# Late stores, diagonal copies, k and v in parts, and other zero products in an attention and MLP kernel

## The chip, the core and the metric

One core of one Trainium2 chip. The time is that of the whole program on the device, in microseconds (us), as the median of several executions. Engine names: PE is TensorE, PEld its weight loads, DVE VectorE, ACT ScalarE, POOL GpSimd, SPq the queue that issues DMAs. L68 and L74 are helpers that record nearly every VectorE, ScalarE and GpSimd operation (L68) and nearly every product (L74), so one goes by the names of tiles.

## The reference

Landmark attention on 8 batches of 8 heads (576 positions of 64, 32 landmarks), then a two-layer network with a layer norm and a residual on the 4608 rows of 512 that come out. What matters here is the inverse of the 32 x 32 matrix of each head, by six Newton steps:

```python
A, Bm, C = sm(q, k_lm), sm(q_lm, k_lm), sm(q_lm, k)
Z = Bm.T / (norm1(Bm) * norminf(Bm) + 1e-6)          # for each head
for _ in range(6):
    Z = 2 * Z - Z @ Bm @ Z
x = A @ Z @ C @ v                                    # then x + relu(ln(x) @ w1) @ w2
```

## The kernel before

The two parts run interleaved: while one set of batches goes through the attention, the rows of earlier batches go through the network ("MLP"), in groups. A product of the MLP is a long row of 128x128x512 matmuls (psh, pso), and these fill TensorE. The Newton steps are short and depend on each other, so each one is set between stretches of MLP products. A step of a set of W units (four heads each) is this (cut: reshapes, and `bmbd`, a second block diagonal that is built after the last step; the first batch multiplies 32x32 blocks and needs no `ebd`):

```python
for it in range(6):
    lo = 0 if it < 5 else LM                                   # LM = 32, D = 64
    psn = p1([P, W, LM + D], "psn")                            # PSUM
    for w in range(W):
        MM(psn[:, w, lo:], ebd[:, w, :, :], st[:, w, lo:])     # four heads in one product
    stn = asm.tile([P, W, LM + D], FP16, name="st", tag="st")
    dve.scalar_tensor_tensor(out=stn[:, :, lo:], in0=st[:, :, lo:], scalar=2.0,
                             in1=psn[:, :, lo:], op0=ALU.mult, op1=ALU.subtract)
    st = stn
    if it < 5:
        ebd = diagonal("ebd", st[:, :, 0:LM], W, masks(W))
    # ... products of the scores, and (by "yield") products of the MLP ...
```

`ebd` is the block diagonal of four 32x32 matrices that lie on four quarters of the partitions. It is made by one multiplication with a mask:

```python
def diagonal(name, src, W, mask):
    t = asm.tile([P, W, 4, LM], FP16, name=name, tag=name, bufs=1)
    dve.tensor_tensor(out=t[:], in0=src[:, :, None, :].broadcast_to([P, W, 4, LM]),
                      in1=mask, op=ALU.mult)
    return t
```

Meanwhile GpSimd converts the next q, k and v to 16 bits (nat, natv) and adds q up to landmarks (asum). At the beginning TensorE has nothing to do until the first loads have landed, and is kept busy with products of zeros (in this trace they start 107 ns apart up to 5.2 us and 56 ns apart after it, and the granted clock is full from 5.2 us on):

```python
def warm(n, cols):
    idle = psM.tile([P, 512], FP32, name="idle", tag="pm")
    for _ in range(n):
        MM(idle[:, 0:cols], zeros[:], zeros[:, None, :].broadcast_to([P, cols // P, P]))
# ...
warm(50, 128)
```

The softmax here doesn't subtract the row's maximum and nothing guards it: scores larger than these inputs give would overflow.

Of the kernel before, what the change touches and what calls it, by code (L numbers as in the profile page):

```python
# [9 lines left out]
FP16 = mybir.dt.float16  # L10
# [3 lines left out]
ALU = mybir.AluOpType  # L14
AX = mybir.AxisListType

P = 128
# [3 lines left out]
def kernel(  # L21
# [55 lines left out]
    def TR(o, i_, idn):  # L77
        keep(nc.tensor.matmul(o, i_, idn, is_transpose=True, tile_position=(0, 0)))


    def load(src, b, u, queue):
        t = stage.tile([P, 2, NJ, D], FP32, name="stg", tag="stg")
        keep(queue.dma_start(
            out=t[:],
            in_=src[b, 4 * u:4 * u + 4].rearrange("(r e) (t j) d -> (e t) r j d", e=2, j=NJ)))
        return t
# [3 lines left out]
    def load_qk(b):  # L90
        for u in range(U):
            raw[b]["q", u] = load(q, b, u, nc.sync)
            raw[b]["k", u] = load(k, b, u, nc.sync)

    def load_v(b):
        for u in range(U):
            raw[b]["v", u] = load(v, b, u, nc.sync)

# [11 lines left out]
    def cast_qk(b, u, nm, engine):  # L110
        t = nat.tile([P, NJ, 2, D], FP16, name="nat", tag="nat")
        engine.tensor_copy(out=t[:].rearrange("p j r d -> p r j d"), in_=raw[b][nm, u][:])
        nat_tiles[b, nm, u] = t
# [51 lines left out]
    maskw = const.tile([P, 4, 4], FP16, name="maskw")  # L165
    mask16 = const.tile([P, 4], FP16, name="mask16")
    nc.gpsimd.tensor_copy(out=mask16[:], in_=mask4[:])
    for w in range(4):
# [21 lines left out]
    pool.tensor_copy(out=natv_buf[0][:, 0:2, :, 0:D], in_=raw[0]["v", 0][:])  # L190
    pool.tensor_copy(out=natv_buf[0][:, 2, :, 0:D], in_=raw[0]["v", 1][:, 0])
    bones = const.tile([P, 4, 32], FP16, name="bones")
    for u in range(U):
# [87 lines left out]

    def diagonal(name, src, W, mask):
        t = asm.tile([P, W, 4, LM], FP16, name=name, tag=name, bufs=1)
        dve.tensor_tensor(out=t[:], in0=src[:, :, None, :].broadcast_to([P, W, 4, LM]),
                          in1=mask, op=ALU.mult)
        return t

    def masks(W):
        return mask16[:, None, :, None].broadcast_to([P, W, 4, LM])


    def attention(bs):
# [13 lines left out]
        for w, (b, u) in enumerate(units):  # L306
            for i, nm in enumerate(("q", "k")):
                n16 = nat_tiles[b, nm, u]
                pst = p2([P, NJ, P], FP16, "pst")

                def sums():
                    for j in range(NJ):
                        MM(pss[:, i, w, :], n16[:, j, :, :].rearrange("p r d -> p (r d)"),
                           pm16[:], start=(j == 0), stop=(j == NJ - 1), skip=True)

                last = (w, i) == (W - 1, 1)
                if last:
                    sums()
                for j in range(NJ):
                    TR(pst[:, j, :], n16[:, j, :, :].rearrange("p r d -> p (r d)"), ident16[:])  # L320
                t = aprep.tile([P, NJ, P], FP16, name="xT", tag="xT" + nm, bufs=5 if nm == "q" else 4)
                if not first and i == 1:
                    dve.tensor_copy(out=t[:], in_=pst[:])
                elif not (first and last):
                    scalar.copy(t[:], pst[:])
                xT[nm, w] = t
                if not last:
                    sums()
                yield
# [10 lines left out]
        if first:  # L340
            dve.tensor_copy(out=t[:], in_=pst[:])
        yield
# [34 lines left out]
        psse_ = p1([P, 4, W * LM], "psse")  # L377
        psse = psse_[:, 0:2, :].rearrange("p a (u l) -> p a u l", u=W)
        for w in range(W):
            for h in range(4):  # L380
                sl = ds(32 * h, 32)
                MM(psse[sl, 1, w, :], bmT[sl, w, :], bmT[sl, w, :], rb=32 * h, cb=32 * h)
        MM(psse[:, 0, :, :], bones[:].rearrange("p a c -> p (a c)"), bm16[:])
        dve.tensor_reduce(out=psse_[:, 2, 0:W], in_=psse[:, 0, :, :], axis=AX.X,
# [9 lines left out]
        if not first:  # L394
            ebd = diagonal("ebd", st[:, :, 0:LM], W, masks(W))

# [3 lines left out]
        for w, (b, u) in enumerate(units):  # L400
            natv = natv_of[b]
            for j in range(NJ):
                for h in range(4):
                    r, e = divmod(h, 2)
                    rows = ds(64 * e, 64)
                    MM(pscv[ds(32 * h, 32), w, :], ect[w][rows, j, ds(32 * r, 32)],
                       natv[rows, 2 * u + r, j, :], rb=64 * e, cb=32 * h,
                       start=(j == 0), stop=(j == NJ - 1), skip=True)
        rcv = asm.tile([P, W], FP32, name="rcv", tag="rcv")
# [7 lines left out]
        for it in range(6):  # L417
# [16 lines left out]
            if not first and it < 5:  # L434
                ebd = diagonal("ebd", st[:, :, 0:LM], W, masks(W))
            if it < W:
# [168 lines left out]
    def attention2(bs, c):  # L605
# [39 lines left out]
        for w in range(W):  # L645
            for h in range(4):
# [11 lines left out]
                                op=ALU.mult)  # L658
        ebd = diagonal("ebd", st[:, :, 0:LM], W, masks(W))


        pscv = ps2.tile([P, 2, 512], FP32, name="pscv", tag="p2")
        for y in range(W // 2):
# [13 lines left out]
            if y + 1 < W // 2:  # L677
                yield
        v_used.update(c.bs)
        pcv = pscv[:, :, 0:(W // 2) * (D + 1)].rearrange("p x (y e) -> p y x e", e=D + 1)  # L680
        rcv = asm.tile([P, W], FP32, name="rcv", tag="rcv")
# [10 lines left out]
        for it in range(6):  # L692
# [9 lines left out]
            if it < 5:  # L702
                ebd = diagonal("ebd", st[:, :, 0:LM], W, masks(W))
            else:
                bmbd = diagonal("bmbd", bm16, W,
                                maskw[:, 0:W, :, None].broadcast_to([P, W, 4, LM]))
            if it < W // 2:
# [168 lines left out]
    def mlp():  # L876
        for g in range(NGRP):
# [44 lines left out]
            for u in range(4):  # L922
# [5 lines left out]
                for m in range(MCH):  # L928
# [4 lines left out]
                    if g == 0 and u >= 2 and m % 8 == 3:  # L933
                        n = len(turned.get(1, ()))
                        if 4 + n in xn_of:
# [4 lines left out]
                                         in1=x_blk.pop(j)[:], op0=ALU.mult, op1=ALU.add)  # L940
                store(j, ot)
                yield True

    stream = mlp()

    def fill(n):
        for _ in range(n):
            if not next(stream, False):
                return


# [5 lines left out]

    warm(50, 128)
    for _ in range(4):
        run(a0)  # L960
        warm(3, 256)
    run(a0)
    warm(1, 512)
    run(a0)
    scalar.copy(natv_buf[0][:, 3, :, 0:D], raw[0]["v", 1][:, 1])
    warm(1, 512)
# [71 lines left out]
    for i, _ in enumerate(a1):  # L1038
        fill(5 if i < 9 else 7)
        settle()  # L1040
        next_cast()
        if 5 <= i < 11:
            sets[0].next_job()
# [8 lines left out]
    for c, after, count in zip(sets, sets[1:] + [None], counts):  # L1052
        for step, _ in enumerate(attention2(c.bs, c)):
            fill(count[step])
            settle()
            if late and step >= 3:
# [6 lines left out]
        while after and (after.jobs or after.lms):  # L1063
            fill(8)
            next_cast()
            after.next_job()
    for _ in stream:
        pass

# [29 lines left out]
```

## Time and profile before

| | before |
|---|---|
| time, median of 3 (range) | 329.57 us (328.33 to 330.2) |
| PE busy, products recorded | 96% of the span, 3409 |
| first psn; first product of MLP group 3 | 15.31 us; 141.71 us |
| waits of psn and its weight load on ebd | 1.6 + 4.4 us |

The prediction below shows the lines for this, and places from the timeline (start us, us, engine, line, operation, out<-in). This is from the page's list of costliest groups; after the count come busy time in us, mean ns of one, and idle time of the engine before them:

```profile
L68 DVE TENSOR_TENSOR ebd<-st,mask 128x256 f16<-128x256 f16 (+1 forms) x30 | 20.7, 690 | 1.0
```

And this is one place from the timeline of the kernel before (start us, us, engine, line, operation, out<-in):

```profile
47.55 1.15 POOL L68 CAST nat<-stg 128x1152 f16<-128x1152 f32 x1 [0.90 <-DMA stg<-in_k_dram]
48.11 0.86 DVE L68 TENSOR_TENSOR ebd<-st,mask 128x256 f16<-128x256 f16 x1
48.97 1.15 POOL L68 CAST nat<-stg 128x1152 f16<-128x1152 f32 x1 [0.27 <-DVE ebd L68]
```

The half-size ebd takes 0.42 us where GpSimd is idle. Here it starts inside a GpSimd cast that runs until 48.70, and ends 0.27 us after it: it takes 0.86 us, since it waits for the cast. That the next cast starts when ebd has ended doesn't show that GpSimd waits too: 0.26 to 0.29 us lie between two casts here also where no ebd is in the way (before 50.40 in this kernel). Where GpSimd did wait is seen in the additions that the prediction lists.

### The profile page before, as it was taken

Reading aid. Unit: us, or ns where it says so; the run is one execution under the profiler, and the core shown is the slowest. Engines: PE = TensorE matmul, PEld = TensorE weight load, DVE = VectorE, ACT = ScalarE, POOL = GpSimd, SP = SyncE. Lnnn points to the kernel's source line nnn. Section 1 sums busy time; section 2 is a strip of 40 time slices with the busy share of each in tenths; the row PEclk is TensorE's granted clock in tenths of the full one; section 3 lists DMA queues with packets and bytes.
Section 4 is the critical chain, followed back from the end, with each engine's and each line's share of the span. In section 5 each row is a group of like instructions: output and inputs, shape, how many; then the busy total and the mean of one; then the engine's idle time right before and its main releaser. Section 6 shows DMA issues by size and latency. Waiting matters only on the chain.

```text
span 327.9 us, 8249 instructions
## 1 busy us (share of the span) xinstructions
PE 314.7 (96%) x3409; PEld 162.3 (50%) x3409; DVE 175.7 (54%) x395; ACT 152.7 (47%) x307; POOL 153.3 (47%) x241
## 2 busy tenths in 40 slices
PE   8889999999999999989999999999999999999995
PEld 8547864553445444435544445454444444444444
DVE  3668769779964797953237668722566120010012
ACT  3546762749960661957204672454046107305600
POOL 3389979999999999999800034100014000000000
PEclk9999999999999999999999999999999999999998
DMA  7999999898797864695022103330242126032023
GB/s 278 394 356 365 366 402 303 297 345 239 241 195 231 234 169 127 156 290 102 4 68 66 34 20 76 82 50 2 64 104 26 32 64 98 0 72 60 0 49 79
DMA packets 36397, 50.34 MB, mean 154 GB/s; under 512 B 17796, under 2 KB 22152, under 8 KB 36360
## 3 DMA queue, kind: packets, MB, share of 16 engines
q1 hardware_dynamic: 36200, 49.69, 52.7%
q8 instruction: 26, 0.43, 0.5%
q10 hardware_dynamic: 160, 0.13, 0.2%
q14 instruction: 11, 0.09, 0.1%
HBM read 36.70 MB, written 9.44 MB: 141 GB/s over the span
## 4 chain that ended last, share of the span: by engine, by line
PE 56%; POOL 22%; DMA 7%; issue 2%; ACT 2%; DVE 1%; SPq 0%; POOLq 0%
PE psh L74 26%; PE pso L74 25%; POOL asum L68 11%; POOL nat L68 6%; POOL natv L68 3%; DMA stg<-in_q_dram 3%; POOL xn L68 2%; DMA w2stg<-in_moe_w_ch_dram 2%; POOL s L68 1%; PE psy L74 1%; PE pscv L74 1%; DMA stg<-in_v_dram 1%; DMA stg<-in_k_dram 1%; DMA xnT<-xn 1%; ACT xn L68 1%
## 5 line engine op out<-in xcount | busy, mean ns | idle before, releaser
L74 PE MATMUL psh<-xnT,w 128*128 128x512 f16 (+1 forms) x640 | 133.7, 358 | 1.4 <-DMA xnT<-xn 1.4
L74 PE MATMUL pso<-w,hT 128*128 128x512 f16 (+1 forms) x592 | 132.9, 374 | 0.0
L68 ACT ACTIVATE hT<-psh 128x512 f16<-128x512 f32 x144 | 84.9, 597 | 97.6 <-PE psh L74 97.4
L74 PEld LDWEIGHTS <-w 128*128 128x128 f16 x640 | 59.5, 98 | 56.7 <-issue 3.1
L74 PEld LDWEIGHTS <-hT 128*128 128x128 f16 x592 | 56.1, 98 | 57.2 <-issue 0.8
L68 DVE SCALAR_TENSOR_TENSOR ot<-pso,rstd,xblk 128x512 f32<-128x512 f32 (+1 forms) x37 | 27.1, 732 | 77.6 <-PE pso L74 77.4
L68 POOL CAST nat<-stg 128x1152 f16<-128x1152 f32 x28 | 32.5, 1167 | 3.4 <-DMA stg<-in_k_dram 1.7
L68 POOL TENSOR_TENSOR asum<-asum 128x256 f32<-128x256 f32 (+2 forms) x54 | 28.4, 527 | 4.2
L68 DVE TENSOR_TENSOR xblk<-psy,rcpd 128x512 f32<-128x512 f32 (+1 forms) x40 | 27.6, 691 | 1.8 <-POOL w L68 0.2
L68 POOL TENSOR_TENSOR asum<-nat 128x576 f32<-128x576 f16 x18 | 23.4, 1299 | 1.5
L68 POOL TENSOR_SCALAR xn<-xblk,mvg 128x512 f16<-128x512 f32 x14 | 9.6, 694 | 30.9 <-ACT junk L68 30.9
L68 DVE SCALAR_TENSOR_TENSOR st<-st,psn 128x192 f16<-128x192 f16 (+3 forms) x36 | 14.2, 395 | 17.6 <-PE psn L74 17.4
L68 POOL CAST natv<-stg 128x1152 f16<-128x1152 f32 (+1 forms) x16 | 17.6, 1119 | 9.6 <-DMA stg<-in_v_dram 9.6
L68 POOL TENSOR_SCALAR negm<-mvg 128x1 f32<-128x1 f32 x14 | 2.7, 191 | 40.5 <-DVE mvg L68 35.9
L68 DVE TENSOR_TENSOR ebd<-st,mask 128x256 f16<-128x256 f16 (+1 forms) x30 | 20.7, 690 | 1.0
L68 DVE STREAM_TRANSPOSE xT<-nat 128x576 uint32<-128x576 uint32 x24 | 18.2, 760 | 2.2 <-POOL nat L68 2.2
L74 PE MATMUL psy<-zcbd,ea 128*128 128x260 f16 (+1 forms) x80 | 15.9, 276 | 1.0 <-DVE xblk L68 0.4
L68 ACT ACTIVATE ea<-psea 128x576 f16<-128x576 f32 x12 | 7.2, 648 | 16.5 <-PE psea L74 16.5
L74 PE MATMUL idle<-zeros 128*128 128x128 f16 (+2 forms) x82 | 13.4, 312 | 1.1 <-DVE eps_ln L172 1.1
L74 PEld LDWEIGHTS <-ea 128*128 128x128 f16 (+1 forms) x80 | 7.1, 100 | 12.2 <-issue 3.5
L68 ACT ACTIVATE junk<-xblk 128x512 f16<-128x512 f32 x14 | 8.8, 625 | 9.4 <-DVE xblk L68 9.2
L68 DVE BATCH_NORM_STATS2 st<-xblk 128x6 f32<-128x512 f32 x18 | 12.4, 688 | 0.5
(115 smaller groups left out, 263.0 us busy)
## 6 DMA issues: line engine op xcount, KB each, us to landing
stg<-in_q_dram SPq DMA_DIRECT2D x16, 576.0 KB, 6.0
stg<-in_k_dram SPq DMA_DIRECT2D x16, 576.0 KB, 5.7
out_dram<-ot SPq DMA_DIRECT2D x70, 128.0 KB, 2.4
stg<-in_v_dram SPq DMA_DIRECT2D x10, 576.0 KB, 6.4
w1stg<-in_moe_w_ch_dram SPq DMA_DIRECT2D x16, 256.0 KB, 6.0
w2stg<-in_moe_w_ch_dram SPq DMA_DIRECT2D x16, 256.0 KB, 5.2
stg<-in_v_dram SPq DMA_DIRECT2D x12, 288.0 KB, 5.5
xnT<-xn SPq DMA_TRANSPOSE x28, 3.3
```

What stands on the lines that cost most here:

```text
L68: return lambda *args, **kw: keep(getattr(self.engine, op)(*args, **kw))
L74: keep(nc.tensor.matmul(o, l, r, start=start, stop=stop, tile_position=(rb, cb), skip_group_check=(skip or cb != 0)))
```

## The change

Its intent, as I read it: shorter VectorE work in the Newton steps (plain copies into a matrix whose other blocks stay zero, instead of a multiplication over all four blocks), stores that don't stand in front of the transposes on the DMA queue, an earlier start, and fewer instructions for the warm-up. The core of the diff (cut: the changed order of some products of the first batch, the casts and copies of the last k and v in parts, the earlier `bmbd`, three more zero products left out after the first batch's steps and one shortened, and the bookkeeping of the stores):

```diff
+halves = ((slice(0, 2), slice(0, 5)), (slice(0, 2), slice(5, NJ)))
+pairs = ((slice(0, 1), slice(0, NJ)), (slice(1, 2), slice(0, NJ)))
-            raw[b]["k", u] = load(k, b, u, nc.sync)
+            raw[b]["k", u] = load(k, b, u, nc.sync, halves if (b, u) == (0, U - 1) else whole)
-            raw[b]["v", u] = load(v, b, u, nc.sync)
+            raw[b]["v", u] = load(v, b, u, nc.sync, pairs if (b, u) == (0, U - 1) else whole)
 ...
+    ebd = const.tile([P, 4, 4, LM], FP16, name="ebd")
+    nc.gpsimd.memset(ebd[:], 0.0)
 ...
-    def diagonal(name, src, W, mask):
-        t = asm.tile([P, W, 4, LM], FP16, name=name, tag=name, bufs=1)
-        dve.tensor_tensor(out=t[:], in0=src[:, :, None, :].broadcast_to([P, W, 4, LM]),
-                          in1=mask, op=ALU.mult)
-        return t
+    def diagonal(src, W):
+        for h in range(4):
+            rows = ds(32 * h, 32)
+            dve.tensor_copy(out=ebd[rows, 0:W, h, :], in_=src[rows, :, :])
 ...
-                store(j, ot)
+                if at_end:
+                    store(j, ot)
+                else:
+                    to_store.append((j, ot))      # stored after the next transposes are issued
 ...
-    warm(50, 128)
+    warm(25, 256)
```

More of the change, by code (lines that the diff above doesn't have):

```diff
@@ L78, in TR, with load @@
         keep(nc.tensor.matmul(o, i_, idn, is_transpose=True, tile_position=(0, 0)))
-    def load(src, b, u, queue):
+    whole = ((slice(0, 2), slice(0, NJ)),)
+    halves = ((slice(0, 2), slice(0, 5)), (slice(0, 2), slice(5, NJ)))
+    pairs = ((slice(0, 1), slice(0, NJ)), (slice(1, 2), slice(0, NJ)))
+    def load(src, b, u, queue, parts=whole):
         t = stage.tile([P, 2, NJ, D], FP32, name="stg", tag="stg")
-        keep(queue.dma_start(
-            out=t[:],
-            in_=src[b, 4 * u:4 * u + 4].rearrange("(r e) (t j) d -> (e t) r j d", e=2, j=NJ)))
+        rows = src[b, 4 * u:4 * u + 4].rearrange("(r e) (t j) d -> r (e t) j d", e=2, j=NJ)
+        for r, j in parts:
+            if parts is halves:
+                for i in range(2):
+                    keep(queue.dma_start(out=t[:, i, j, :], in_=rows[i][:, j, :]))
+            else:
+                keep(queue.dma_start(out=t[:, r, j, :],
+                                     in_=rows[r][:, :, j, :].rearrange("r p j d -> p r j d")))
         return t
@@ L111, in cast_qk @@
         t = nat.tile([P, NJ, 2, D], FP16, name="nat", tag="nat")
-        engine.tensor_copy(out=t[:].rearrange("p j r d -> p r j d"), in_=raw[b][nm, u][:])
+        for _, j in halves if (b, u, nm) == (0, U - 1, "k") else whole:
+            engine.tensor_copy(out=t[:, j, :, :].rearrange("p j r d -> p r j d"),
+                               in_=raw[b][nm, u][:, :, j, :])
         nat_tiles[b, nm, u] = t
@@ L165 @@
     maskw = const.tile([P, 4, 4], FP16, name="maskw")
-    mask16 = const.tile([P, 4], FP16, name="mask16")
-    nc.gpsimd.tensor_copy(out=mask16[:], in_=mask4[:])
+    ebd = const.tile([P, 4, 4, LM], FP16, name="ebd")
+    nc.gpsimd.memset(ebd[:], 0.0)
     for w in range(4):
@@ L191 @@
     pool.tensor_copy(out=natv_buf[0][:, 2, :, 0:D], in_=raw[0]["v", 1][:, 0])
+    pool.tensor_copy(out=natv_buf[0][:, 3, 5:NJ, 0:D], in_=raw[0]["v", 1][:, 1, 5:NJ])
     bones = const.tile([P, 4, 32], FP16, name="bones")
@@ L279, in warm @@
             MM(idle[:, 0:cols], zeros[:], zeros[:, None, :].broadcast_to([P, cols // P, P]))
-    def diagonal(name, src, W, mask):
-        t = asm.tile([P, W, 4, LM], FP16, name=name, tag=name, bufs=1)
-        dve.tensor_tensor(out=t[:], in0=src[:, :, None, :].broadcast_to([P, W, 4, LM]),
-                          in1=mask, op=ALU.mult)
-        return t
-    def masks(W):
-        return mask16[:, None, :, None].broadcast_to([P, W, 4, LM])
+    def diagonal(src, W):
+        for h in range(4):
+            rows = ds(32 * h, 32)
+            dve.tensor_copy(out=ebd[rows, 0:W, h, :], in_=src[rows, :, :])
     def attention(bs):
@@ L309, in attention, with sums @@
                 pst = p2([P, NJ, P], FP16, "pst")
-                def sums():
-                    for j in range(NJ):
+                def sums(js=range(NJ)):
+                    for j in js:
                         MM(pss[:, i, w, :], n16[:, j, :, :].rearrange("p r d -> p (r d)"),
@@ L316, in attention @@
                 last = (w, i) == (W - 1, 1)
-                if last:
+                if last and not first:
                     sums()
-                for j in range(NJ):
-                    TR(pst[:, j, :], n16[:, j, :, :].rearrange("p r d -> p (r d)"), ident16[:])
+                for js in (range(0, 5), range(5, NJ)) if first and last else (range(NJ),):
+                    if first and last:
+                        sums(js)
+                    for j in js:
+                        TR(pst[:, j, :], n16[:, j, :, :].rearrange("p r d -> p (r d)"),
+                           ident16[:])
                 t = aprep.tile([P, NJ, P], FP16, name="xT", tag="xT" + nm, bufs=5 if nm == "q" else 4)
@@ L325, in attention @@
                     scalar.copy(t[:], pst[:])
+                else:
+                    scalar.copy(t[:, 0:5, :], pst[:, 0:5, :])
                 xT[nm, w] = t
@@ L340, in attention @@
         if first:
-            dve.tensor_copy(out=t[:], in_=pst[:])
+            dve.tensor_copy(out=t[:, 5:NJ, :], in_=pst[:, 5:NJ, :])
         yield
@@ L378, in attention @@
         psse = psse_[:, 0:2, :].rearrange("p a (u l) -> p a u l", u=W)
+        MM(psse[:, 0, :, :], bones[:].rearrange("p a c -> p (a c)"), bm16[:])
         for w in range(W):
@@ L382, in attention @@
                 MM(psse[sl, 1, w, :], bmT[sl, w, :], bmT[sl, w, :], rb=32 * h, cb=32 * h)
-        MM(psse[:, 0, :, :], bones[:].rearrange("p a c -> p (a c)"), bm16[:])
         dve.tensor_reduce(out=psse_[:, 2, 0:W], in_=psse[:, 0, :, :], axis=AX.X,
@@ L394, in attention @@
         if not first:
-            ebd = diagonal("ebd", st[:, :, 0:LM], W, masks(W))
+            diagonal(st[:, :, 0:LM], W)
         v_used.update(bs)
@@ L401, in attention @@
             natv = natv_of[b]
-            for j in range(NJ):
-                for h in range(4):
-                    r, e = divmod(h, 2)
-                    rows = ds(64 * e, 64)
-                    MM(pscv[ds(32 * h, 32), w, :], ect[w][rows, j, ds(32 * r, 32)],
-                       natv[rows, 2 * u + r, j, :], rb=64 * e, cb=32 * h,
-                       start=(j == 0), stop=(j == NJ - 1), skip=True)
+            order = [(j, h) for j in range(NJ) for h in range(4)]
+            if first and w == W - 1:
+                order.sort(key=lambda jh: jh[1] // 2)
+            for j, h in order:
+                r, e = divmod(h, 2)
+                rows = ds(64 * e, 64)
+                MM(pscv[ds(32 * h, 32), w, :], ect[w][rows, j, ds(32 * r, 32)],
+                   natv[rows, 2 * u + r, j, :], rb=64 * e, cb=32 * h,
+                   start=(j == 0), stop=(j == NJ - 1), skip=True)
         rcv = asm.tile([P, W], FP32, name="rcv", tag="rcv")
@@ L434, in attention @@
             if not first and it < 5:
-                ebd = diagonal("ebd", st[:, :, 0:LM], W, masks(W))
+                diagonal(st[:, :, 0:LM], W)
             if it < W:
@@ L658, in attention2 @@
                                 op=ALU.mult)
-        ebd = diagonal("ebd", st[:, :, 0:LM], W, masks(W))
+        diagonal(st[:, :, 0:LM], W)
         pscv = ps2.tile([P, 2, 512], FP32, name="pscv", tag="p2")
@@ L679, in attention2 @@
         v_used.update(c.bs)
+        bmbd = asm.tile([P, W, 4, LM], FP16, name="bmbd", tag="bmbd", bufs=1)
+        dve.tensor_tensor(out=bmbd[:], in0=bm16[:, :, None, :].broadcast_to([P, W, 4, LM]),
+                          in1=maskw[:, 0:W, :, None].broadcast_to([P, W, 4, LM]), op=ALU.mult)
         pcv = pscv[:, :, 0:(W // 2) * (D + 1)].rearrange("p x (y e) -> p y x e", e=D + 1)
@@ L702, in attention2 @@
             if it < 5:
-                ebd = diagonal("ebd", st[:, :, 0:LM], W, masks(W))
-            else:
-                bmbd = diagonal("bmbd", bm16, W,
-                                maskw[:, 0:W, :, None].broadcast_to([P, W, 4, LM]))
+                diagonal(st[:, :, 0:LM], W)
             if it < W // 2:
@@ L940, in mlp @@
                                          in1=x_blk.pop(j)[:], op0=ALU.mult, op1=ALU.add)
-                store(j, ot)
+                if at_end:
+                    store(j, ot)
+                else:
+                    to_store.append((j, ot))
                 yield True
     stream = mlp()
+    to_store, at_end = [], []
     def fill(n):
@@ L949, in fill, with work @@
                 return
+    def work(n):
+        k = len(to_store)
+        fill(n)
+        settle()
+        for _ in range(k):
+            store(*to_store.pop(0))
     a0, a1 = attention((0,)), attention((1,))
@@ L956, in run @@
             next(a)
-    warm(50, 128)
-    for _ in range(4):
+    warm(25, 256)
+    for i in range(4):
         run(a0)
-        warm(3, 256)
+        if i < 3:
+            warm(3, 256)
     run(a0)
-    warm(1, 512)
+    warm(1, 128)
     run(a0)
-    scalar.copy(natv_buf[0][:, 3, :, 0:D], raw[0]["v", 1][:, 1])
+    scalar.copy(natv_buf[0][:, 3, 0:5, 0:D], raw[0]["v", 1][:, 1, 0:5])
     warm(1, 512)
@@ L1038 @@
     for i, _ in enumerate(a1):
-        fill(5 if i < 9 else 7)
-        settle()
+        work(5 if i < 9 else 7)
         next_cast()
@@ L1053 @@
         for step, _ in enumerate(attention2(c.bs, c)):
-            fill(count[step])
-            settle()
+            work(count[step])
             if late and step >= 3:
@@ L1063 @@
         while after and (after.jobs or after.lms):
-            fill(8)
+            work(8)
             next_cast()
             after.next_job()
+    at_end.append(True)
     for _ in stream:
-        pass
+        while to_store:
+            store(*to_store.pop(0))
 _INS = ['q', 'k', 'v', 'moe_g_ln', 'moe_w_ch1', 'moe_w_ch2']
```

## The prediction

Two words in it. The lock, which the expectations further down call the port, is a name for what keeps VectorE and GpSimd apart in waits (0.86 us in place of 0.42); the traces show the waits, not what lies behind them. An operation is unheld when it starts before the one in front of it has ended, as the second rcpd does by 0.08 us. Its scaling at 30.03 takes 0.34 us, and the GpSimd scaling beside it 0.63 us, where those around that one take 0.47 to 0.51.

> **What bounds the kernel now.** I read the page's first two parts, then the chain of waits, then the timeline at the one place where TensorE truly waits, then the Newton steps of the attention, because four of the five edits land on these.[...]
>
> ```profile
> PE 314.7 (96%) x3409; PEld 162.3 (50%) x3409; DVE 175.7 (54%) x395; ACT 152.7 (47%) x307; POOL 153.3 (47%) x241
> PE   8889999999999999989999999999999999999995
> POOL 3389979999999999999800034100014000000000
> PE 56%; POOL 22%; DMA 7%; issue 2%; ACT 2%; DVE 1%; SPq 0%; POOLq 0%
> ```
>
> TensorE is busy from end to end, and the digits show two regimes: up to about slice 19 (160 us) GpSimd is as full as TensorE; after that it is nearly idle. The chain agrees: from the end back to 141.7 us it is matmuls, before that mostly GpSimd (22%). So after 141.7 us only fewer or shorter matmuls would help, and the diff leaves the products there as they are. Before it, two full engines run side by side and meet at one point:
>
> ```profile
> 133.82 1.22 SPq L870 DMA_TRANSPOSE xnT<-xn  x1
> 135.09 0.57 SPq L106 DMA_DIRECT2D stg<-in_q_dram  x1
> 135.75 1.20 SPq L870 DMA_TRANSPOSE xnT<-xn  x1
> 137.04 1.24 SPq L829 DMA_DIRECT2D out_dram<-ot  x2
> 138.38 1.25 SPq L870 DMA_TRANSPOSE xnT<-xn  x1
> 141.71 1.89 PE L74 MATMUL psh<-xnT,w 128*128 128x512 f16 x8 [1.42 <-DMA xnT<-xn]
> ```
>
> These are the DMA queue and TensorE around the first product of MLP group 3. TensorE stands still for 1.42 us until the last of four transposes has landed. Its input was ready at about 136.2 (two xn end there), but two stores (1.24 us of issue) stood in front of it. The other real waits of TensorE between 30 and 142 us, by releaser:
>
> ```profile
> PE psn L74 <- DVE ebd L68: 1.6, 3, 0.7
> PE psh L74 <- DMA xnT<-xn: 1.4, 1, 1.4
> PE psec L74 <- DVE xblk L68: 0.6, 2, 0.4
> ```
>
> psn is the product of a Newton step, and ebd the block diagonal that VectorE builds for it. With the waits of its weight load added (4.4 us in 7), the start-to-start gaps of the matmuls give about 2.3 us of standstill on ebd inside the steps between 40 and 123 us. The worst one, as the timeline has it:
>
> ```profile
> 118.50 1.27 POOL L68 TENSOR_TENSOR asum<-nat 128x576 f32<-128x576 f16 x1
> 118.58 1.74 DVE L68 TENSOR_TENSOR ebd<-st,mask 128x512 f16<-128x512 f16 x1
> 120.37 0.34 PE L74 MATMUL psn<-st,ebd 128*128 128x96 f16 x4 [0.70 <-DVE ebd L68]
> ```
>
> The same ebd takes 691 ns where GpSimd is idle (424 ns for the half-size one). Here it started just after a GpSimd addition and ended 0.55 us after that addition did: it waited for it.
>
> [...] ebd above, and the scaling of w at 27.61, which takes 0.58 us beside GpSimd and 0.34 us at 30.03, where it got there first. [...]
>
> ```profile
> 128.58 0.78 DVE L68 STREAM_TRANSPOSE xT<-nat 128x576 uint32<-128x576 uint32 x1 [2.19 <-POOL nat L68]
> 129.39 0.21 DVE L68 RECIPROCAL rcpd<-psy 64x8 f32<-64x8 f32 x1
> 208.26 0.75 DVE L68 SCALAR_TENSOR_TENSOR ot<-pso,rstd,xblk 128x512 f32<-128x512 f32 x1
> 208.93 0.19 DVE L68 RECIPROCAL rcpd<-psy 64x8 f32<-64x8 f32 x1
> ```
>
> The first rcpd works on partitions 64 to 127 and starts 0.03 us after the end of its predecessor; the second works on 0 to 63 and starts 0.08 us before it. [...] the opening zero products come every 107 ns up to about 4.8 us, then every 56.
>
> **The change part by part.**
>
> Zero products: 25 x 256 columns are the 6400 columns of 50 x 128. At half clock that is the same time, so the warm-up still ends near 5.8 us, when the first cast (done at 5.3) is waiting. Worth 0.0 to 0.1 us. [...]
>
> Last k in four DMAs, v in two: the cast of the last k is 0.76 us from 9.41 and everything waits for it. With half of it done while the rest lands, about 0.4 us go (the second cast 0.36 us, estimated by elements). Of the last v, one head pair can be cast earlier and the other is shared by ScalarE and GpSimd (0.68 us becomes about 0.4). The two gains lie one behind the other only in part, since both meet in the first psn at 15.31. The DMAs are full from 2.2 us on, and the extra issues (about 0.4 us each) don't starve them. Sum: -0.4 us at 15 us, and I carry it to 140 us on TensorE.
>
> Late stores: between the last two transposes of group 3 the instruction order of the changed kernel has one half store instead of two, so the last is issued 0.6 us sooner. Small by itself, but on the only long wait.
>
> Diagonal copies: each ebd (30 of them, 424 to 1740 ns) becomes four copies of 32 partitions. Small VectorE operations take 0.16 to 0.22 us; [...] I count 4 x 0.19 + 3 x 0.03, so 0.85 us, and 0.95 us from the end of st to psn with both hand-overs. What TensorE allows from the end of st to the next psn, standstill excluded, read from starts and ends: batch 1: 1.00, 1.00, 0.54, 0.54, 0.53 us; batch 2: 1.33, 0.96, 0.13, 0.65, 0.76; batches 3 and 4: 1.58, 1.92, 1.19, 0.97, 0.75; later sets mostly over 1.1. The excess of 0.95 over these is 1.2 + 1.3 + 0.2 = 2.7 us against 2.3 now: +0.5. GpSimd gains: in the set of batches 3 and 4 its additions beside an ebd or bmbd took 0.33 to 0.43 us longer, six times, 2.1 us; [...] perhaps 1.3 us of it comes back. The earlier bmbd takes one operation off the last step.
>
> Sum: TensorE now arrives at group 3 at 140.1 us and goes on at 141.7. Then: arrival 140.1 - 0.4 + 0.5 = 140.2; transposes landed 141.6 - 0.6 - 1.3 = 139.7. It goes on at 140.2, 1.5 us sooner; the 187 us after it don't change. 329.57 - 1.5 = 328.1.
>
> **The rivals.**
>
> A, the copies overlap: 0.5 us per step. The excess falls to 0.4 us (-1.9), TensorE arrives at 137.8 and waits for the transposes until about 139.0 to 139.7: 327.0. For it: small unheld operations on VectorE follow at 0.07 us. Against: the two rcpd above.
>
> C, one lock wait per diagonal, as ebd has now, about 0.4 us on average on top of the serial copies: 1.35 us per step, excess 7.2 us (+4.9), arrival 144.6, 332.5.
>
> D, the lock changes hands after each copy. VectorE's two scalings at 25.75 did this: 1.05 us for the pair, each ending just after a GpSimd one. GpSimd's row for a q is 1.14, 1.27, 0.73, 0.46, 0.32, 0.32 us with gaps of 0.08; four copies would need about 1.7 us (estimate). Excess 12.7 us (+10.4), arrival 150.1, 338. For it: the trace, plainly. Against: it would have cost enough that a tuner would scarcely keep it; and the gaps may let two copies pass.
>
> E, the stores now stand behind transposes that wait for GpSimd, output buffers run out, VectorE's ot waits and TensorE with it. There are four buffers and an ot every 3.5 us at most, some 14 us of room: under 0.5 us.
>
> **Range and chances.** I give A 0.30, the sum above 0.30, C 0.23, D 0.17. The middle of this is **328.3 us**. Low end 325.3 (A with a better start and all of GpSimd's 2.1 us), high end 336.5 (most of D). Over 2% faster is below 323.1: it needs more than all waits before 142 us, 0.03. Over 2% slower is above 336.2, only D: 0.17. Within 2%: 0.80.
>
> **What would show it.** Right: first psn near 14.9; the wait for xnT at 140 us gone or under 0.5 us; the matmuls after it shifted as a block; copies in fours at about 0.2 us; GpSimd's additions at 0.73 and 0.32 throughout. Wrong: copies of 0.5 us and more between 40 and 125 us and waits for ebd above 6 us in total (C or D); copies that start before the one ahead has ended (A); a start that is not earlier, if the smaller pieces of k land later.

## The result, and the profile after

The changed kernel takes 343.44 us (342.05 to 346.01, 6 runs), beside 329.64 us (328.33 to 330.2, 6 runs) for the kernel before. It is slower: 1.044 times, 95% interval 1.039 to 1.049. The predicted 328.3 us and its range of 325.3 to 336.5 are both missed.

The page of the changed kernel:

```profile
PE 318.1 (93%) x3381; PEld 161.4 (47%) x3381; DVE 196.4 (57%) x486; ACT 153.3 (45%) x308; POOL 151.0 (44%) x242
...
PE   7799976987699997899999999999999999999995
...
PEclk9969999999899999999999999999999999999999
...
PE 70%; DVE 17%; issue 2%; ACT 2%
...
L68 DVE COPY ebd<-st 32x64 f16<-32x64 f16 (+1 forms) x120 | 40.4, 336 | 2.3
```

TensorE has lost 9s in several slices up to the 17th (145 us), and only there. The clock has two dips (slices 3 and 11). GpSimd is gone from the chain of waits, and VectorE has 17% in place of 1%. The 120 copies take 40.4 us where the 30 multiplications took 20.7: 336 ns each, not 190.

The waits, by releaser (us in total, times, longest), for what the prediction showed as 1.6 us in 3, and 4.4 us in 7:

```profile
PEld L74 <- issue: 19.0, 49, 1.5
PEld L74 <- DVE ebd L68: 17.9, 15, 3.3
...
PE psn L74 <- DVE ebd L68: 11.7, 12, 2.8
```

A product and its weight load wait for the same ebd (at 120.37 us in the kernel before, both start when it is there), so the two ebd rows overlap. To count once, I take from the trace, for each first product of a Newton step, the gap from the start of the matmul before it, less the time that this matmul itself needs. In the first three sets of steps with an ebd (40 to 123 us before, 45 to 139 us in the changed kernel) this standstill is 13.9 us in the changed kernel and 2.3 before; over the whole run it is 14.7 and 4.1. The latter measure is used below. It has a floor: another choice of the time that a matmul needs lowers all of its values by 0.7 to 1.2 us, to 0.0 in the last two kernels of the table below, so only its differences count.

The place from before, in the timeline of the changed kernel:

```profile
48.02 1.67 DVE L68 COPY ebd<-st 32x64 f16<-32x64 f16 x4
48.14 1.15 POOL L68 CAST nat<-stg 128x1152 f16<-128x1152 f32 x1 [0.89 <-DVE st L68]
49.53 1.16 POOL L68 CAST nat<-stg 128x1152 f16<-128x1152 f32 x1 [0.25 <-DMA stg<-in_k_dram]
49.75 0.26 PE L74 MATMUL psn<-st,ebd 128*128 128x96 f16 x2 [0.60 <-DVE ebd L68]
```

The first copy starts at 48.02 while GpSimd is idle. Then GpSimd's cast gets in, and a copy stands until it ends at 49.29; the rest follow in GpSimd's gap. This is no single case: of the 76 copies up to 172 us, 31 take over 0.25 us, and each of the 31 ends 0.03 to 0.06 us after a GpSimd instruction does. The longest wait of TensorE:

```profile
85.23 4.41 POOL L68 CAST natv<-stg 128x1152 f16<-128x1152 f32 x4
87.00 2.86 DVE L68 COPY ebd<-st 32x64 f16<-32x64 f16 x4
...
89.92 0.34 PE L74 MATMUL psn<-st,ebd 128*128 128x96 f16 x2 [2.77 <-DVE ebd L68]
...
91.04 0.73 DVE L68 COPY ebd<-st 32x64 f16<-32x64 f16 x4
```

Four casts back to back leave no gap, and the four copies last 2.86 us (in the trace three of them are 0.49, 1.08 and 1.08 us, the last 0.18). TensorE stands for 2.77 us. A little later, with GpSimd idle, the same four take 0.73 us. That is the serial time the prediction counted on.

There is a second loss, at the start, which the prediction took to be a gain. The timeline of TensorE before:

```profile
14.24 0.47 PE L74 MATMUL pscv<-natv,ect 64*32 64x65 f16 x36 [0.31 <-POOL natv L68]
...
15.31 0.26 PE L74 MATMUL psn<-st 32*32 32x96 f16 x8
```

and after:

```profile
13.34 0.84 PE L74 MATMUL pscv<-natv,ect 64*32 64x65 f16 x62
15.56 0.33 PE L74 MATMUL pscv<-natv,ect 64*32 64x65 f16 x10 [1.38 <-issue]
...
16.48 0.26 PE L74 MATMUL psn<-st 32*32 32x96 f16 x8
```

In the changed kernel 62 of 72 products go through early (13.34), as intended. Then TensorE stands for 1.38 us, and what ends it is "issue": nothing that the profile shows as a wait. Something does run then. In the DMA view of the changed kernel from 13.0 to 13.3 us there is this row (packets, MB, share):

```profile
q8 instruction: 1, 0.02, 21.0%
```

One packet of 16 KB, started at 13.23 us and 1.0 us long in the trace. Both kernels have 26 of these. In the kernel before, the first starts at 10.94 us, and no product of the burst that follows waits on issue. A packet of 16 KB in a queue called "instruction", and a stop that the semaphores don't explain, make a refill of TensorE's instructions the suspect. The counts fit: from the first of the 26 packets to the last, TensorE starts 6298 matmuls and weight loads in the kernel before and 6240 in the changed one, so 252 and 250 to a packet, though single packets lie 104 to 433 of them apart. The last three packets start after the same number of them in both kernels (6051, 6311 and 6559, counted in the two traces), some 20 us later in the changed one. So these packets go with the count of TensorE's instructions. Whether they cost anything is the question here. Each product brings a weight load with it (3409 of each before), so the 25 fewer products at the beginning are 50 fewer instructions in front of everything that follows; three more products go a little later (3381 in place of 3409 in all).

Third, the clock. These are rows of the table of stretches, for 17 to 24 us, first of the changed kernel, then of the one before (the stretch and its length, the busy us and instructions of PE, PEld, DVE, ACT and POOL, then the granted clock, the DMA share and GB/s):

```profile
17.00:24.00 7.00, 7.00 (x77) 2.57 (x70) 2.90 (x9) 1.97 (x4) 6.24 (x10) 0.54 1.09 353
```

```profile
17.00:24.00 7.00, 5.89 (x74) 2.83 (x73) 4.50 (x11) 2.62 (x7) 6.12 (x10) 1.00 1.10 354
```

Shortly after the stop at 14 us, TensorE runs at half clock for some 7 us. It does so again from 89.2 us on for 3.4 us, from within the stop of 2.77 us. But the clock isn't the main loss: one of the six runs of the changed kernel had a mean clock of 1.0, and it took 342.05 us.

### The profile page after: what moved, and what is told of

Same layout as the page of the kernel before. It is cut to its first block, busy times and chain, and to the rows that moved or that the text cites. A ratio compares the mean times of both kernels' runs of the same rounds, so it can differ in the third digit from the quotient of the medians. Undisturbed runs are those within 1.5% of the kernel's fastest.

```text
span 341.9 us, 8290 instructions
## 1 busy us (share of the span) xinstructions
PE 318.1 (93%) x3381; PEld 161.4 (47%) x3381; DVE 196.4 (57%) x486; ACT 153.3 (45%) x308; POOL 151.0 (44%) x242
## 4 chain that ended last, share of the span: by engine, by line
PE 70%; DVE 17%; issue 2%; ACT 2%
PE pso L74 31%; PE psh L74 30%; DVE ebd L68 7%; PE pscv L74 3%; DVE st L68 2%; DVE xT L68 2%; PE psy L74 2%; DVE xblk L68 1%; DVE lmk L68 1%; ACT xn L68 1%; PE psn L74 1%; DVE ot L68 1%; PE psec L74 1%; PE psea L74 1%; DVE rcpd L68 0%
## 5 line engine op out<-in xcount | busy, mean ns | idle before, releaser
L74 PE MATMUL psh<-xnT,w 128*128 128x512 f16 (+1 forms) x640 | 135.3, 360 | 0.0
L68 DVE COPY ebd<-st 32x64 f16<-32x64 f16 (+1 forms) x120 | 40.4, 336 | 2.3
L68 POOL TENSOR_TENSOR asum<-asum 128x256 f32<-128x256 f32 (+2 forms) x54 | 27.4, 507 | 4.2
L68 POOL TENSOR_TENSOR asum<-nat 128x576 f32<-128x576 f16 x18 | 23.0, 1278 | 1.5
L68 POOL CAST natv<-stg 128x1152 f16<-128x1152 f32 (+2 forms) x17 | 17.9, 1075 | 8.3 <-DMA stg<-in_v_dram 8.3
L74 PE MATMUL psn<-st,ebd 128*128 128x96 f16 (+1 forms) x84 | 8.5, 207 | 11.8 <-DVE ebd L68 11.7
L74 PEld LDWEIGHTS <-ebd 128*128 128x128 f16 x84 | 5.7, 98 | 21.5 <-DVE ebd L68 17.9
L74 PE MATMUL idle<-zeros 128*128 128x256 f16 (+2 forms) x54 | 13.9, 379 | 1.1 <-DVE eps_ln L184 1.1
L68 ACT ACTIVATE ea<-psea 128x576 f16<-128x576 f32 x12 | 7.1, 648 | 16.8 <-PE psea L74 16.8
L68 DVE BATCH_NORM_STATS2 st<-xblk 128x6 f32<-128x512 f32 x18 | 12.4, 688 | 0.5
```

The lines of the kernel that those rows point to most:

```text
L68: return lambda *args, **kw: keep(getattr(self.engine, op)(*args, **kw))
L74: keep(nc.tensor.matmul(o, l, r, start=start, stop=stop, tile_position=(rb, cb), skip_group_check=(skip or cb != 0)))
```

## The experiments

Two theories of the main loss. The theory: VectorE and GpSimd exclude each other in these operations (at the port, as it is called here), and a diagonal of four copies asks for the port four times, where one multiplication asks once. The rivals: the copies are innocent and the loss lies in the start, the refills and the clock; or what hurts is only that four operations in four quarters of the partitions run one after the other. All ten kernels gave the right result. The kernel before ran beside each set: 329.94, 329.92 and 329.19 us.

| run | time, us | ratio to before (95%) | ebd: standstill of TensorE, us |
|---|---|---|---|
| before (profile of the start) | 329.57 | | 4.1 |
| changed kernel | 343.44 | 1.044 (1.039 to 1.049) | 14.7 |
| a_masked | 332.17 | 1.007 (1.003 to 1.012) | 3.8 |
| b_copies | 342.21 | 1.039 (1.036 to 1.042) | 16.8 |
| a_warm50 | 342.44 | 1.039 (1.035 to 1.043) | 18.7 |
| b_warm25 | 334.27 | 1.012 (1.006 to 1.018) | 3.3 |
| b_reduce4 | 331.07 | 1.004 (1.001 to 1.007) | 7.0 |
| b_scale4 | 339.27 | 1.029 (1.026 to 1.032) | 16.6 |
| a_masked_warm50 | 330.0 | 1.000 (0.998 to 1.003) | 7.4 |
| b_pad | 329.22 | 0.998 (0.996 to 0.9995) | 5.1 |
| b_psmask | 326.91 | 0.993 (0.991 to 0.994) | 1.2 |
| best_psmask | 326.42 | 0.991 (0.990 to 0.993) | 1.2 |

### a_masked: the change without the copies

```diff
-        for h in range(4):
-            rows = ds(32 * h, 32)
-            dve.tensor_copy(out=ebd[rows, 0:W, h, :], in_=src[rows, :, :])
+        dve.tensor_tensor(out=ebd[:, 0:W, :, :],
+                          in0=src[:, :, None, :].broadcast_to([P, W, 4, LM]),
+                          in1=mask16[:, None, :, None].broadcast_to([P, W, 4, LM]), op=ALU.mult)
```

(`mask16` is made again, and the zeroing of `ebd` goes.)

> The changed kernel, with the block diagonal of the Newton step built as before it: one masked multiplication of 128 partitions by VectorE in place of four copies of 32. Theory 'the port changes hands after each copy': the traces put 13.9 us of TensorE's standstill on ebd inside the steps in the changed kernel and 2.3 us before, so about 11 us come back here: 331 to 333 us, and the standstill falls to 2 to 4 us. Rival 'the copies are innocent and the loss is the start, the instruction fetches and the clock': 342 to 344 us. If the half-clock stretches at 89 us follow from the standstill there, they go with it.

332.17 us, and a standstill on ebd of 3.8 us. So 11.3 us of the 13.8 lost are the copies', and the standstill fell by about as much (14.7 to 3.8). The rest of the change still costs 2.2 us. Both half-clock stretches are gone from its profile; another of 3.4 us, from 72.6 us on, lies behind a stop on issue of 2.50 us.

### b_copies: the kernel before, with the copies alone

The reverse edit: the kernel before, whose `diagonal` makes four copies into a constant tile set to zero once.

> The kernel before, with one part of the change alone: the four copies of 32 partitions build ebd. Theory of the port: the same standstill as in the whole change, some 11 us more than before: 338 to 341 us. Rival (copies innocent): 329 to 331 us. The copies should show as in the changed kernel: about 0.18 us each and about 0.01 us from the end of one to the start of the next, with starts that wait for the end of a GpSimd operation between 40 and 125 us.

342.21 us, slightly more than expected: 12.3 us above the kernel before. The copies alone do nearly all of it, and they do it in the kernel without any other edit. Their mean is 329 ns, and their standstill 16.8 us is even larger than in the whole change. The four runs have a mean clock of 0.988 to 0.995, the kernel before 0.998 to 1.0; what this adds isn't separated (the run with 0.995 was the slowest of the four, 343.44 us).

### b_reduce4: four operations in four quarters, but no copies

The diff is against b_copies; `bmbd` is built as before in both.

```diff
-            dve.tensor_copy(out=ebd_c[rows, 0:W, h, :], in_=src[rows, :, :])
+            dve.tensor_reduce(out=ebd_c[rows, 0:W, h, :], in_=src[rows, :, :, None],
+                              axis=AX.X, op=ALU.max)        # a maximum over one element: a copy
```

> The kernel before, ebd built in four operations on the same four quarters as in the change, but as maxima over an axis of length one in place of copies: same starts in another quarter, same one SBUF input, but an operation that is not a copy[...]. Theory 'each copy asks for the port that GpSimd holds': no start waits for the end of a GpSimd operation, each starts about 0.01 us after the one before it has ended, four take 0.7 to 0.9 us throughout: 329 to 331.5 us. Rival 'what hurts is that four operations in four quarters run one after the other': as with the copies, 340 to 343 us.

The timeline of this kernel at the known place:

```profile
49.13 0.88 DVE L68 TENSOR_REDUCE ebd<-st 32x64 f16<-32x64 f16 x4
49.18 1.15 POOL L68 CAST nat<-stg 128x1152 f16<-128x1152 f32 x1 [0.26 <-PE psh L74]
...
50.07 0.26 PE L74 MATMUL psn<-st,ebd 128*128 128x96 f16 x2 [0.27 <-DVE ebd L68]
```

All four ran while a GpSimd cast was running, in 0.88 us, and the cast took its normal 1.15 us. The same quarters, the same data, the same order, and 331.07 us in place of 342.21. So the other 11 us come with the operation being a copy. Four maxima take 0.88 us beside a cast, four copies 1.67; why a copy waits for GpSimd and a maximum doesn't isn't shown. The 1.2 us that are left over the kernel before are a net figure: the four maxima run one after the other (0.88 us, and 1.15 us in the sets of four units, where 0.7 to 0.9 were expected throughout), but they are also free of the waits for the port that the multiplication has (its two forms average 548 and 901 ns in the kernel before, and take 424 and 691 where GpSimd is idle). b_psmask below, free of them too, with one operation, is 3.4 us faster than this (2.3 us under its kernel before, where b_reduce4 is 1.15 us over).

### b_scale4: four operations on all partitions

```diff
+        for h in range(4):
+            dve.tensor_scalar(out=ebd_c[:, 0:W, h, :], in0=src, scalar1=mask4[:, h:h + 1],
+                              scalar2=None, op0=ALU.mult)
```

> The kernel before, ebd built in four multiplications by a column of the mask, each on all 128 partitions, so none starts in another quarter than the one before; each has one SBUF input [...]. Theory 'each operation asks for the port anew': if GpSimd gets the port between any two, starts stand behind GpSimd operations as with the copies, 338 to 342 us. Rival 'GpSimd gets in only because a held copy starts after the one before it has ended': starts 0.07 us apart, one wait for each diagonal at most, 329 to 331 us.

```profile
49.18 1.67 DVE L68 TENSOR_SCALAR ebd<-st,mask 128x64 f16<-128x64 f16 x4
49.67 1.15 POOL L68 CAST nat<-stg 128x1152 f16<-128x1152 f32 x1 [0.22 <-DMA stg<-in_q_dram]
```

339.27 us. None of these starts in another quarter than the one before, and none is held: each starts 0.08 to 0.09 us before the end of the one before it, where a copy starts 0.01 us after. Still four of them last 1.67 us beside casts: the first stands until the cast before has ended (0.30 us), the fourth takes 1.16 us, since the cast at 49.67 got in before it. GpSimd gets in between two VectorE instructions that follow at once. The rival that it gets in only where a copy starts after the end of the one before falls. What counts here is how many instructions take the port, not how they follow each other.

### a_warm50, b_warm25 and b_pad: the zero products

a_warm50 is the changed kernel with `warm(50, 128)`, b_warm25 the kernel before with `warm(25, 256)`. b_pad is the kernel before with 50 instructions again, but of other sizes:

```diff
-    warm(50, 128)
+    for _ in range(25):
+        MM(idle[:, 0:192], zeros[:], zeros[:, None, 0:96].broadcast_to([P, 2, 96]))
+    for _ in range(25):
+        MM(idle[:, 0:16], zeros[:], zeros[:, 0:16])
```

The theory of the fetch in the expectations: each refill, a 16 KB packet of the instruction queue, goes with the count of TensorE's instructions (252 and 250 to a packet in the two traces above, the last three at the same counts), so with fewer of them in front it comes at a later place of the work.

> The changed kernel with 50 zero products of 128 columns again: the same columns, 50 more instructions on TensorE (with the weight loads). Theory of the fetch: [...] in the changed kernel one falls into the scores at 14 us (1.4 to 1.5 us that the trace calls issue) and two more at 43 and 76 us (1.0 and 1.5); shifted back by 50 instructions they fall where they did before and cost nothing: 339 to 341 us, first Newton product near 15.0 us in place of 16.48. Rival (the late start is the smaller pieces of k and v, or the zero products' columns): 343 to 344 us, and the first Newton product stays at 16.4.

> The kernel before with 25 zero products of 256 columns alone. Theory of the fetch: stops of 1 to 1.5 us that the trace calls issue appear in TensorE's stream at new places, 331 to 333 us. Rival (the change of the zero products is worth 0.0 to 0.1 us, as predicted): 329.5 us and no such stops over 0.5 us.

> The kernel before with 25 zero products of 192 columns and then 25 of 16 columns: 50 instructions as before, but other sizes and 5200 columns in place of 6400. Theory 'it is the number of TensorE's instructions, which moves the refills of its instructions': no stop of 0.9 us that the trace calls issue at 15 us, and 329.3 to 330.5 us, like before. Rival 'it is the size of the products or what they do to the clock': 332 to 335 us, like 25 products of 256 (334.3).

b_warm25 alone loses 4.3 us: 334.27, more than the 331 to 333 expected. Its profile has three stops of TensorE on issue, each inside a burst of 72 pscv products, before 15.6, 72.2 and 108.6 us (0.77, 2.05 and 0.56 us); a 16 KB packet of the instruction queue started 1.6, 0.3 and 1.7 us before TensorE stopped (13.21, 69.84 and 106.27 us in the trace). Its first psn is at 16.48 us, exactly as in the changed kernel. b_pad, with as many instructions as before but 5200 columns instead of 6400, takes 329.22 us. The timeline of b_pad:

```profile
13.72 1.10 PE L74 MATMUL pscv<-natv,ect 64*32 64x65 f16 x72
...
15.42 0.26 PE L74 MATMUL psn<-st 32*32 32x96 f16 x8
```

All 72 products in one go, no stop (one of 0.70 us comes in a later burst, before 106.2 us). So it is the number of instructions, not the size or the columns. The kernel before is one in which the refills happen to fall in good places, and taking 50 instructions from the front moves them (the first from 10.94 us to 13.23 in the changed kernel and 13.21 in b_warm25). In a_masked, which has 25 zero products too, the stop in the first burst is back, and one of 2.50 us before 71.8. How long a stop lasts can be read from the traces. In the changed kernel, a_masked, b_warm25 and b_pad there are ten stops on issue over 0.25 us in pscv bursts, and each of them ends 2.3 to 2.7 us after the start of the last 16 KB packet. I read a stop as what is left of this time when TensorE has come to the end of the instructions it has, which no view shows directly: 2.50 us in a_masked, where the packet starts at 69.27 us and TensorE stops at 69.28; 0.56 us in b_warm25, where it starts 1.7 us before.

a_warm50 was a half miss. The first psn is at 15.05 us, as expected, and the stops of the changed kernel in the pscv bursts (1.38 us before 15.6, 1.30 before 77.7) are gone from this profile; but the time fell by 1.0 us, not by 2 to 4: 342.44, and the intervals of the two kernels overlap, so even this isn't shown. The standstill on ebd is 18.7 us in this kernel, 4.0 more than in the changed one. So the gain at issue was given back at the port; that TensorE comes earlier to a GpSimd that isn't earlier would explain it, but wasn't tested. With the copies gone, the same edit is worth 2.2 us (a_masked against a_masked_warm50, whose intervals in the table just touch).

The half clock goes with the stops: each dip in these profiles before the last microseconds begins in one or up to 2.0 us behind it. The profiled run of b_warm25 has no dip and took 331.06 us at a clock of 0.997; its other three runs have 0.99 to 0.995 and took 333.6 to 335.8. So whether the clock falls after a stop differs from run to run of the same kernel.

The traces show more of this. In all twelve the clock changes only on a grid of 3.41 us: from its first opening to each later change it is a whole number of these (94, or 320.85 us, in the kernel before; in the changed one the stretches between changes last 13.65, 6.83, 64.85, 3.41 and 249.17 us, that is 4, 2, 19, 1 and 73), and a dip lasts one or two. Up to 318 us, the six stretches of this grid at full clock in which TensorE was idle longest, 1.96 to 2.98 us, were each followed by half clock. Those with 1.85 us or less were not, but for one: 14.13 to 17.54 us in the changed kernel, with 1.43 us idle and else small products; whether small products count for less stays open. The stop of 2.05 us in b_warm25 is cut in two by the grid (1.48 us in the larger part) and had no dip; 2.07 us within one stretch had (85.81 to 89.22 us in the changed kernel). The grid lies elsewhere in each run (first opening at 3.9 to 7.0 us), which would explain the differences between runs; only one run of each kernel has a trace, so this isn't shown.

### a_masked_warm50: both undone

> The changed kernel with both undone, the copies and the 25 zero products: what is left are the late stores and the last k and v in parts. From the start of the first Newton product of the changed kernel with 50 zero products (15.05 us against 15.31 before, 0.26 us sooner) and the 0.6 us sooner transposes at group 3: 328.5 to 329.3 us, that is 0.6 to 1.0 us under the kernel before. Rival (the rest of the change costs something too): over 330 us, as the changed kernel with the masked diagonal alone has 332.2.

330.0 us, where 328.5 to 329.3 were expected: neither better nor worse than before (1.000). The first psn is at 15.06 us, 0.25 us sooner than before, but the standstill on ebd is 7.4 us in its profile, against 4.1. The late stores and the loads in parts gain nothing that could be measured on this base. It completes the sum, in this order of undoing: copies 11.3 us (343.44 to 332.17), zero products 2.2 us (332.17 to 330.0; with the three left out later still missing), the rest 0.0. In the other order it is 1.0 and 12.4.

### b_psmask and best_psmask: the port taken away

If the second SBUF input is what makes the multiplication ask for the port, the mask can come from PSUM. It fits beside psn in its bank:

```diff
+        psn_ = p1([P, 512], "psn")
+        psn = psn_[:, 0:W * (LM + D)].rearrange("p (w c) -> p w c", w=W)
+        MM(psn_[:, 508:512], ident16[:], mask16[:])            # once per set
         for it in range(6):
             lo = 0 if it < 5 else LM
-            psn = p1([P, W, LM + D], "psn")
 ...
-                ebd = diagonal("ebd", st[:, :, 0:LM], W, masks(W))
+                ebd = diagonal("ebd", st[:, :, 0:LM], W,
+                               psn_[:, None, 508:512, None].broadcast_to([P, W, 4, LM]))
```

> The kernel before, with the mask of the block diagonal read from PSUM in place of SBUF (one product of 128x4 puts it beside psn in its bank, once per set): still one masked multiplication per ebd, on 128 partitions and as long, but with one SBUF input in place of two. Theory of the port: it no longer waits for GpSimd nor GpSimd for it; ebd is 0.69 or 0.42 us throughout, with no end just after that of a GpSimd operation; the waits of TensorE on ebd (6.0 us in both rows before) fall to about 2, GpSimd's additions in the set of batches 3 and 4 are 0.73 and 0.32 us throughout: 327 to 329 us. Rival (the second SBUF input was not what cost the port, or the read from PSUM is slower): 329.5 us or more, and ebd still ends with GpSimd operations.

> The same mask in PSUM in the changed kernel with both costly parts undone (masked diagonal, 50 zero products; the late stores and the last k and v in parts stay). Theory of the port: 330.0 us of that kernel less its waits on ebd (11.9 us in both rows, some 7 of standstill, of which about 5 go), part of which the wait for the transposes at group 3 takes back: 326 to 328.5 us, under the kernel before. Rival: 329.5 to 330.5 us.

The first ebd of each set (5 of 30) keeps its mask in SBUF. Two views of b_psmask, the timeline at the known place and the groups by form:

```profile
47.48 1.15 POOL L68 CAST nat<-stg 128x1152 f16<-128x1152 f32 x1 [0.91 <-DMA stg<-in_k_dram]
...
48.00 0.42 DVE L68 TENSOR_TENSOR ebd<-st,psn 128x256 f16<-128x256 f16 x1
```

```profile
L68 DVE TENSOR_TENSOR ebd<-st,psn 128x512 f16<-128x512 f16 x10 | 6.9, 686 | 0.3
L68 DVE TENSOR_TENSOR ebd<-st,psn 128x256 f16<-128x256 f16 x15 | 6.3, 421 | 0.5
```

The ebd at 48.00 lies wholly inside a cast, and takes 0.42 us. All 25 of these take what they take alone (686 and 421 ns; in the kernel before the two forms average 901 and 548). The standstill is 1.2 us, the floor of the measure. 326.91 us, 0.7% under the kernel before and a little better than expected; with the late stores and the loads in parts 326.42 us, 0.9% under it. The 0.5 us between the two agrees with what the prediction hoped of those parts, but the intervals overlap, so it isn't shown.

## Why the prediction was wrong

Point by point, in its own order.

The zero products, "Worth 0.0 to 0.1 us": wrong. The half of the argument that was given holds (the columns don't matter: b_pad), but it left out that fewer instructions move the refills. Cost: 4.3 us alone in the kernel before, 2.2 in the changed kernel without the copies, 1.0 (not clear of noise) with them. A slip beside it: the opening products ran at half speed up to 5.2 us, not 4.8.

The last k and v in parts, "-0.4 us at 15 us": with 50 zero products the first psn is at 15.06 us against 15.31 before, so 0.25 us, or nearer 0.4 beside the other kernels with the old start (15.35 to 15.55 us). So the size was about right; the shorter zero products and the new order of the first batch weren't separated from it. In the changed kernel the stop at 14 us turned it into +1.2.

Late stores, "0.6 us sooner": not to be seen in the changed kernel, where TensorE comes too late at group 3 to wait. In a_masked_warm50 one half store stands between the last two transposes, as foreseen, and the last is issued 1.95 us after the one before it in place of 2.63. But that one was itself 0.7 us later (136.44 against 135.75 us), so the last starts when it did (138.39 against 138.38), and what it feeds starts later (142.56 against 141.71). Why it took longer to land isn't shown.

The diagonal copies, "I count 4 x 0.19 + 3 x 0.03, so 0.85 us": this is the step that failed. The serial order is real (a copy starts 0.01 us after the end of the one before), and 0.73 to 0.79 us is what four take without a port to wait for. But the count has no wait for GpSimd in it, although the prediction's own lines show what such a wait costs an ebd (1.74 us in place of 0.69) and a scaling (0.58 us in place of 0.34), and its rival D counts it for the copies. Measured: 1.67, 1.72 and 2.86 us per diagonal beside GpSimd, +11.3 us in all in place of +0.5. Four serial operations that don't wait for the port still ended 1.2 us above the kernel before (b_reduce4). Rival A, copies that overlap, falls with the same starts.

GpSimd's gain, "perhaps 1.3 us of it comes back": the size came. The asum rows went from 527 to 507 ns (54 of them) and from 1299 to 1278 ns (18), 1.5 us in sum over all sets. It was worth nothing, since TensorE arrived later than GpSimd by then.

The rivals. D, "the lock changes hands after each copy", had 1.7 us per diagonal and 338 us. It is what happened. The trace spoke "plainly" for it, and it got a chance of 0.17, because "it would have cost enough that a tuner would scarcely keep it". That is a guess about how the change came to be, set against a reading of the profile. The other reason, that the gaps may let two copies pass, does hold, and isn't enough: casts of 1.15 us with gaps of 0.25 leave room for one or two of four. D was also too small, by 4 us for the copies alone (342.21 us). It had no case like the four casts without a gap.

## What to carry to other kernels

Where the trace shows VectorE operations that end just after GpSimd ones (0.03 to 0.06 us here), count how many of them wait so, not how long each is: four short copies beside a busy GpSimd cost 12.3 us more than one long multiplication (342.21 us against 329.94), and an operation that doesn't wait at all (here the multiplication with its mask in PSUM, 326.91 us) beats both. One SBUF input alone isn't enough: the copies and the scalings of b_scale4 have one, and waited (1.67 us for four of either kind at the place from before). Before removing or adding instructions in front of a dense burst of small products, look where the packets of the instruction queue fall (50 fewer cost the kernel before 4.3 us); an "issue" stop inside such a burst, with such a packet started up to 2.7 us before its end, is the sign. And when the profile speaks for a rival, don't discount it on the ground that nobody would have kept such a change.
